# A staging buffer for transposed activations, three buffers instead of four for unit vectors, and narrower turns of half tiles

## The chip, the cores and the metric

The kernel runs on one core of one Trainium2 chip. The metric is the device time of one execution in microseconds, lower is better. TensorE does the matmuls, VectorE and ScalarE read PSUM and write SBUF, GpSimd (POOL) issues the loads of q, k, v and the weights and does a few additions, and SyncE (SP) issues the other DMAs.

## The reference

Cosine attention over 8 batches of 12 heads, 448 tokens and 64 numbers per head, then a mixing block on the 768 channels. Inputs and the output are float32; the kernel computes in bf16 with float32 sums.

```python
q_n = q / (norm(q) + 1e-6);  k_n = k / (norm(k) + 1e-6)     # q, k, v: (8, 12, 448, 64)
attn = softmax(q_n @ k_n.T / tau)                           # tau = 0.1
x = (attn @ v) -> (8, 448, 768)
u = x + transpose(transpose(x) @ U @ V)                     # U: 448 x 32, V: 32 x 448
out = u + relu(u @ w_ch1) @ w_ch2                           # 768 -> 3072 -> 768
```

## The kernel before

**Work and its tiles.** For each batch, q and k are loaded by thirds of four heads, squared and summed (lines 657 to 665), scaled to unit length (line 733), and transposed on TensorE pair of heads by pair (line 574, 112 columns). The transposed pair goes from PSUM into one of the buffers of `r_qkT` (line 397) by a copy on ScalarE (line 1475) or VectorE (line 1477). Scores are computed in bursts of up to three slots (line 797), exponentials on ScalarE (line 815), the product with v on TensorE (line 842), and its scaling on VectorE (lines 873 and 874), which writes into a tile `X` of the batch. There are two `X` buffers. In batches 2 and later the last quarter of the keys of two pairs is one slot, so that a burst may need three pairs.

`stage0` (line 947) then projects X with U (line 959), copies the 32-wide result A to SBUF, multiplies it with V (line 1012) and adds it to X on VectorE (line 1021): X now holds u. Every 128-token tile of u goes to DRAM twice, because the MLP comes later: as it is (`kept`, line 1050) and transposed (`turned`, line 1060). For the second one, TensorE turns the tile with six transposes of 128 columns (line 574 through `flip`), and a copy on ScalarE or VectorE writes the turned tile over the tile of X that it came from. Two batches make seven tiles, so the middle one (t = 3) is turned in two halves of 64 tokens, one for each batch. Batches 0 and 1 work partly in another way: batch 0's tiles aren't stored at all.

The MLP works on tiles of tokens: uT comes back from DRAM (line 908), u too (line 913). Tiles are taken two at a time, the down projection as seven half-size products (line 1328), the up projection plainly (line 1299) in the first six pairs of tiles and as seven products (line 1192) in the last six. The sums and differences of weights for the seven products live in space that earlier stages have left: `Gone` (line 57) makes them wait until the given-up buffers of the rings have had their last use. `Shrink` (line 37) is a ring that gives up buffers: `r_qkT` has six buffers for the first three batches (`NPAIR * WHOLE` = 18 pairs), and from then on those whose numbers are listed.

**What sets the order.** Nothing is emitted in the order of the source. The kernel records operations (`Op`) with an estimated duration, dependencies, and the ring slots that they take and give back; `Plan.run` (line 196) then walks through time and gives each engine its next operation. TensorE's operations stand in streams with a fixed rank (lines 502 to 512): transposes of q and k, then those of u (`pe_u`), then products with v, ..., scores, and the MLP last. An operation marked `ACT/DVE` goes to whichever of the two engines takes it first, and one marked `fast` waits for VectorE where that is free. So a change of one duration or one buffer changes the order of all engines from that place on, and the split of the shared operations. Each engine then executes its own list strictly in that order, and an operation that has to wait holds all behind it. What it waits for on the chip are the semaphores of the data it touches, not the slots of the plan.

For the turned tiles the plan of the kernel before says: the first transpose depends on the additions to u and on the store of u, `u_adds[x] + made[x][-1:]`. Only the copy, which writes over X, has to wait for that store on the chip.

Of the kernel before, what the change touches and what calls it, by code (L numbers as in the profile page):

```python
# [317 lines left out]
def kernel(  # L318
# [12 lines left out]
    nc = tc.nc  # L331

    B, H, S, D = q.shape
    C = H * D
    R = moe_U.shape[-1]
    F = moe_w_ch1.shape[-1]
    NPAIR = H // 2
    CC = C // 128
    NC = F // 128
    CH = C // 2  # L340
    SC = 4
    SCH = S // SC
# [9 lines left out]
    WHOLE = 3  # L352
# [21 lines left out]
    def fixed_ring(tiles):  # L374
        return Ring(len(tiles), lambda i: tiles[i % len(tiles)])
# [5 lines left out]
            for i in range(3)]  # L381
# [13 lines left out]
    r_inv = ring(4, [SCH, 2, G, SC], FP, "inv")  # L395
    qkT_t = sqk_t[:, 3 * SQ:]
    r_qkT = Shrink([qkT_t[:, 2 * SC * SCH * i:2 * SC * SCH * (i + 1)].rearrange("p (b s) -> p b s", b=2 * SC)
                    for i in range(6)], NPAIR * WHOLE, (2, 3, 4, 5))
    X_t = const.tile([128, 2 * 4 * C], BF, name="X_sb")
    r_X = fixed_ring([X_t[:, 4 * C * i:4 * C * (i + 1)].rearrange("p (t c) -> p t c", t=4) for i in range(2)])  # L400
    A_t = const.tile([128, 3, C], BF, name="A_sb")
# [49 lines left out]
    def bank_ring(groups, cap, shape=None):  # L451
        def make(g):
            if len(g) > 1:
                return bank_t[:, g[0]:g[-1] + 1, :]
            t_ = bank_t[:, g[0], :]
            if shape is not None:
                t_ = t_[:, 0:shape[0] * shape[1]].rearrange("p (a b) -> p a b", a=shape[0])
            return t_
        return BankRing(banks, groups, cap, make)
# [5 lines left out]
    r_z = bank_ring([(7,), (4,), (6,), (5,), (3,), (1,), (2,), (0,)], 4)  # L465
    r_sc = bank_ring([(0, 1), (2, 3), (4, 5)], 3)
    r_low = bank_ring([(5,), (4,), (3,), (2,), (1,), (0,)], 4)
    r_fl = bank_ring([(5,), (4,), (3,), (2,), (1,), (0,), (6,)], 2)
    r_av3 = bank_ring([(5,), (4,), (3,), (2,), (1,), (0,)], 2, (4, D + 8))
    r_av2 = bank_ring([(5,), (4,), (3,), (2,), (1,), (0,), (6,)], 2, (4, D + 8))  # L470
# [7 lines left out]
    r_sc1 = bank_ring([(0,), (2,), (1,), (3,)], 4)  # L478
# [4 lines left out]
    ident = const.tile([128, 128], BF, name="ident")  # L483
# [16 lines left out]
    plan = Plan()  # L500
# [6 lines left out]
    pe_u = plan.stream("PE")  # L507
# [11 lines left out]
    def pe_t(n):  # L519
        return n / 2400.0 + 0.0025  # L520

    def act_t(n, fixed=0.055):
        return fixed + n * 0.00083

    def dve_t(n, fast=1, fixed=0.065):
        return fixed + n * 0.00105 / fast

    def any_t(n, fast=1, fixed=0.065):
        return {"ACT": act_t(n), "DVE": dve_t(n, fast, fixed)}
# [32 lines left out]
    def flip(stream, ins, n, into, part, deps, acq, rel, wide=1, eng="ACT/DVE", took=0.05, ring_=None):  # L562


        tp = Slot(ring_ or r_mm, 1)
        tp.own = True
        for z, x in enumerate(ins):
            def fn(z=z, x=x):
                if z == 0:
                    w = len(ins) // wide  # L570
                    tp.tile = bank_t[:, tp.group[0], :].bitcast(BF)[:, 0:w * n].rearrange(
                        "p (w n) -> p w n", w=w)
                m = 128 // wide
                nc.tensor.transpose(out=tp.tile[m * (z % wide):m * (z % wide + 1), z // wide, :], in_=x(),  # L574
                                    identity=ident[:n, :n])
            o = plan.add(Op("PE", took, fn, deps=deps + [id_set] if z == 0 else (), acq=[tp] + acq,
                            rel=rel if z == len(ins) - 1 else []), stream)
        took = any_t(n * len(ins) // wide, 2)
        c = plan.add(Op(eng, took, None, deps=[o], acq=acq, rel=[tp], prio=0.2, fast=True))

        def move():
            for dst, src in part(into(), tp.tile):
                copy_op(c, dst, src)
        c.fn = move
        return c
# [304 lines left out]
    prev, first_v, made, u_adds, projects = {}, {}, {}, {}, {}  # L890
# [56 lines left out]
    def stage0(b, X, muls):  # L947
        par = b % 2
# [13 lines left out]
        def project_part(c0, c1, mm):  # L962
            for t in range(4):
                project(t, c0, c1, mm)
# [5 lines left out]
        if not by_pe:  # L970
            o = projects[b] = plan.add(Op("PE", 0.2 + 2 * pe_t(CH), project_all, deps=muls + consts[par], acq=mms + [A]), pe_a)
        for (c0, c1), mm in zip(cols, mms):
            need = [m for i, m in enumerate(muls) if i * D < c1]
            if by_pe:
                o = plan.add(Op("PE", 0.2 + pe_t(c1 - c0), lambda c0=c0, c1=c1, mm=mm: project_part(c0, c1, mm),
                                deps=need + consts[par], acq=[mm, A],
                                rel=[warm] if b == 0 and c0 == 0 else []),
                             pe_z[c0 // 128] if b == 0 else pe_a if c1 < C else pe_av)
# [7 lines left out]
        n = 128 * len(tiles)  # L986
# [12 lines left out]
        for jobs in (jobs, wide):  # L999
            for z, i, t, c0, c1 in jobs:  # L1000
# [7 lines left out]
                for y, (AA, col) in enumerate(parts):  # L1008
                    AA.uses += 1
                    AA.left += 1  # L1010
                    o = plan.add(Op("PE", pe_t(c1 - c0), lambda y=y, AA=AA, col=col, c0=c0, c1=c1,
                                    mm=mm, last=len(parts) - 1: nc.tensor.matmul(  # L1012
                        out=mm.tile[:, 0:c1 - c0], lhsT=V_sb[:, col:col + 128],
                        rhs=AA.tile[:, c0:c1], start=(y == 0), stop=(y == last)),
                        deps=(a_done if jobs is wide else [a_done[z]]) if y == 0 else (), acq=[mm] if y == 0 else [], rel=[AA]), pe_a if c1 < C or jobs is wide else pe_av)
# [10 lines left out]
                rel = [mm] + ([prev["X"]] if t == 3 and b == 1 else [])  # L1026
                for s_ in rel[1:]:
# [3 lines left out]
                                         deps=[o], rel=rel, prio=0 if b == 1 else 2))  # L1031
# [11 lines left out]
        for i, t in enumerate(tiles):  # L1043
            x = b // 2, t
            r = slice(64 * par, 64 * par + 64) if t == 3 and b > 1 else slice(0, 128)
            X.uses += 1
            X.left += 1
            u_adds[x] = [o for (z, k), o in adds.items() if k == i]
            made.setdefault(x, []).append(plan.add(Op(
                "SP", 0.1, lambda x=x, r=r, t=t: nc.sync.dma_start(out=kept[x][r, :], in_=X.tile[r, t - 3 * par, :]),  # L1050
                deps=u_adds[x], rel=[X], prio=1 if b == 1 else 0, lat=("x", 1.0, 2.0))))
            if x in turned:
                X.uses += 1
                X.left += 1
                view = lambda t=t: X.tile[:, t - 3 * par, :].rearrange("p (c n) -> p c n", c=CC)
                c = flip(pe_u, [(lambda cc=cc, t=t: X.tile[:, t - 3 * par, 128 * cc:128 * cc + 128]) for cc in range(CC)],
                         128, view, lambda t_, y, r=r: [(t_[:, :, r], y[:, :, r])], u_adds[x] + made[x][-1:], [], [],
                         took=0.056, ring_=r_sc1 if b == 1 else r_fl)
                made_t.setdefault(x, []).append(plan.add(Op(
                    "SP", 0.1, lambda x=x, r=r, view=view: nc.sync.dma_start(  # L1060
                        out=turned[x].rearrange("p (c n) -> p c n", c=CC)[:, :, r], in_=view()[:, :, r]),
                    deps=[c], rel=[X], prio=1 if b == 1 else 0, lat=("x", 1.0, 2.0))))
        prev["A"], prev["X"] = A, X
        return us, uT, ut

# [407 lines left out]
    def copy_op(op, dst, src):  # L1473
        if op.by == "ACT":
            nc.scalar.copy(out=dst, in_=src)  # L1475
        else:
            nc.vector.tensor_copy(out=dst, in_=src)
# [68 lines left out]
    def att(b):  # L1546
        X = Slot(r_X, 0) if b else X0
        muls = [] if b else list(muls0)
        for n, x in enumerate(groups_of(b) if b else ()):
            scores(b, x, first_v.get(b - 1, ()) if n == 0 and b == 2 else ())  # L1550
        for p in range(0 if b else 1, NPAIR):
            if b == 0:
                for c in range(SC):
                    scores(b, [(p, c)])
            muls += values(b, p, X)
        if b < WIDE <= b + 2:
            v_set[b + 2] = [fill(lambda: set_v_tiles(v_t[b % 2]), 1200, prio=3.5, deps=[last_av[b, p] for p in range(NPAIR)])]
        else:
            v_set[b + 2] = v_set[b]
        last_mul.extend(muls)  # L1560
        return stage0(b, X, muls)

    first = lead, [plan.add(Op("SP", 0.45, lambda i=i, src=src: nc.sync.dma_start(
        out=lead.tile[:, i], in_=src[0, 0:2].rearrange("h (s c) d -> s h (c d)", c=SC)),
        acq=[uv], prio=-5, lat=2.5)) for i, src in enumerate((q, k))]
# [8 lines left out]
    for c in range(SC):  # L1574
# [8 lines left out]
                        deps=[zf, *begun], prio=-2, lat=12.0))]  # L1583
# [37 lines left out]
    n = 0  # L1621
# [68 lines left out]
```

## Time and profile before

| | us |
|---|---|
| median of 3 runs (lowest, highest) | 572.73 (572.58, 574.4) |
| the profiled execution | 573.77 |
| its span, first to last instruction | 572.0 |
| TensorE busy | 561.3 |
| VectorE busy | 464.3 |
| ScalarE busy | 306.2 |
| POOL busy | 148.5 |

A row of the profile names the line, the engine, the operation and the tiles, then the time it was busy, the mean duration of one, and the engine's idle time before it with what ended that. Line numbers are those of the kernel before; PE is TensorE, DVE VectorE, ACT ScalarE, SPq SyncE's queue. Line 574 is shared by all transposes, and lines 1475 and 1477 by all copies that either engine may take, so the tile's name and the shape tell them apart. The granted TensorE clock is 1.00 throughout.

### The profile page before, as it was taken

The page shows a single profiled execution, that of the slowest core. Times are in us where ns is not written, and L with a number is a line of the kernel's source. Part 1 is how long each engine was busy: PE and PEld are TensorE (multiplying, and loading weights), DVE is VectorE, ACT ScalarE, POOL GpSimd, SP SyncE. Part 2 cuts the span into 40 slices and gives each one's busy share as a digit, 9 for nine tenths or more (in the row PEclk, how much of TensorE's full clock was granted, in tenths as well). Part 3 has the DMA queues.
Part 4 walks back from the last instruction along what each step waited for, and adds up shares of the span by engine and source line. Part 5 has one row for each costly group of instructions (what it writes and reads, how often), then busy time and mean ns, then how long its engine had stood idle before and what let it go on. Part 6 is the DMA issues. An engine that isn't in the chain of part 4 may idle for free.

```text
span 572.0 us, 16131 instructions
## 1 busy us (share of the span) xinstructions
PE 561.3 (98%) x6721; PEld 412.7 (72%) x6722; DVE 464.3 (81%) x1061; ACT 306.2 (54%) x495; POOL 148.5 (26%) x180
## 2 busy tenths in 40 slices
PE   8899999999999999999999999999999999999996
PEld 6565656768767758767867766876969696969784
DVE  8979859999898989979969976687897776758583
ACT  7977655766567874766865684560404141414140
POOL 8526241002424225124120510001030303030302
PEclk9999999999999999999999999999999999999999
DMA  9999997632968849349645922312124121221201
GB/s 156 204 207 139 210 192 107 144 84 52 105 155 128 87 88 177 64 93 136 95 83 101 131 70 71 112 30 84 30 78 127 37 83 31 83 69 45 79 7 55
DMA packets 116264, 57.61 MB, mean 101 GB/s; under 512 B 72256, under 2 KB 116192, under 8 KB 116192
## 3 DMA queue, kind: packets, MB, share of 16 engines
q0 software_dynamic: 72352, 25.73, 39.8%
q1 hardware_dynamic: 43840, 30.87, 18.8%
q8 instruction: 52, 0.85, 0.6%
q14 instruction: 20, 0.16, 0.1%
HBM read 61.65 MB, written 20.64 MB: 144 GB/s over the span
## 4 chain that ended last, share of the span: by engine, by line
PE 91%; DVE 5%; ACT 1%; DMA 1%; issue 1%; POOL 0%; SPq 0%; DVEq 0%; POOLq 0%
PE bank L1328 28%; PE bank L1299 16%; PE bank L1192 15%; PE bank L842 8%; PE bank L797 6%; PE bank L1411 6%; PE bank L1453 6%; PE bank L574 5%; DVE qk_all L733 2%; PE bank L1012 1%; DVE ss L665 1%; PE bank L959 1%; DMA relu<-in_k_dram 1%; DVE X_sb L1021 0%; DMA out_dram<-relu 0%
## 5 line engine op out<-in xcount | busy, mean ns | idle before, releaser
L815 ACT ACTIVATE attn<-bank 128x896 bf16<-128x896 f32 (+1 forms) x163 | 140.1, 915 | 35.8 <-PE bank L797 35.3
L1328 PEld LDWEIGHTS <-relu 128*128 128x128 bf16 x1008 | 95.5, 98 | 66.2 <-issue 7.7
L1299 PE MATMUL bank<-uT,w_sb 128*128 128x256 bf16 x864 | 106.1, 273 | 1.6 <-ACT relu L1309 1.4
L1328 PE MATMUL bank<-w_sb,relu 128*128 128x384 bf16 x576 | 103.4, 326 | 0.0
L1299 PEld LDWEIGHTS <-w_sb 128*128 128x128 bf16 x864 | 81.0, 98 | 20.3 <-issue 9.9
L665 DVE TENSOR_REDUCE ss<-sqk 112x8 f32<-112x512 bf16 x95 | 62.1, 675 | 3.1 <-ACT sqk L657 2.6
L733 DVE TENSOR_TENSOR qk_all<-qk_all,inv 112x512 bf16<-112x512 bf16 x93 | 60.5, 683 | 0.3
L842 PE MATMUL bank<-v_nat,attn 128*128 128x65 bf16 (+1 forms) x1536 | 58.3, 193 | 0.8 <-DVE X_sb L880 0.6
L842 PEld LDWEIGHTS <-attn 128*128 128x128 bf16 (+1 forms) x1536 | 53.8, 97 | 5.4 <-issue 3.3
L596 POOL DMA_DIRECT2D qk_all<-in_q_dram x24 | 17.7, 738 | 147.9 <-ACT attn L815 49.1
L1309 ACT ACTIVATE relu<-bank 128x512 bf16<-128x512 f32 x48 | 28.7, 598 | 44.1 <-PE bank L1299 43.3
L1192 PEld LDWEIGHTS <-w_sb 128*128 128x128 bf16 x864 | 49.3, 98 | 0.8
L797 PE MATMUL bank<-sqk 64*64 64x448 bf16 (+1 forms) x460 | 46.9, 356 | 0.7 <-ACT sqk L1475 0.5
L1229 ACT COPY attn<-bank 128x512 f32<-128x512 f32 x18 | 10.6, 587 | 65.6 <-PE bank L1192 60.6
L1220 ACT ACTIVATE relu<-relu 128x512 bf16<-128x512 bf16 x36 | 22.7, 630 | 29.7 <-DVE relu L1214 28.8
L1192 PE MATMUL bank<-uT,w_sb 128*128 128x128 bf16 x648 | 38.1, 219 | 0.0
L1353 POOL TENSOR_TENSOR relu<-relu,u_nat 128x384 f32<-128x384 f32 x7 | 8.4, 1205 | 110.0 <-ACT relu L1351 82.7
L1411 PE MATMUL bank<-uT,w_sb 128*128 128x384 bf16 (+1 forms) x288 | 35.6, 273 | 0.0
L619 POOL DMA_DIRECT2D v_nat<-in_v_dram x42 | 31.1, 746 | 17.2 <-DMA w_sb<-in_moe_w_ch_dram 14.6
L1453 PE MATMUL bank<-w_sb,relu 128*128 128x384 bf16 x192 | 35.4, 326 | 0.0
L874 DVE TENSOR_TENSOR X_sb<-bank,rd 128x256 bf16<-128x256 f32 x72 | 30.6, 425 | 2.6 <-DVE rd L873 0.2
L1353 POOL TENSOR_TENSOR attn<-attn,u_nat 128x384 f32<-128x384 f32 x6 | 12.8, 2156 | 69.0 <-ACT attn L1351 69.0
(137 smaller groups left out, 943.2 us busy)
## 6 DMA issues: line engine op xcount, KB each, us to landing
qk_all<-in_q_dram POOLq DMA_DIRECT2D x23, 224.0 KB, 4.2
qk_all<-in_k_dram POOLq DMA_DIRECT2D x23, 224.0 KB, 5.5
u_nat<-u SPq DMA_DIRECT2D x25, 192.0 KB, 2.5
w_sb<-in_moe_w_ch_dram POOLq DMA_DIRECT2D x4, 1152.0 KB, 17.9
w_sb<-in_moe_w_ch_dram POOLq DMA_DIRECT2D x8, 576.0 KB, 15.5
uT<-uT SPq DMA_DIRECT2D x24, 192.0 KB, 3.0
u<-X_sb SPq DMA_DIRECT2D x22, 192.0 KB, 2.0
uT<-X_sb SPq DMA_DIRECT2D x21, 192.0 KB, 3.1
```

Of the source, the lines that this page charges most:

```text
L619: ops = [load(lambda j=j, r0=r0, c=c, s0=s0, s1=s1: nc.gpsimd.dma_start(out=v_t[b % 2][r0:r0 + s1 - s0, :, j, 0:D], in_=src[c, s0:s1]), (s ...
L665: lambda i=i, a0=a0, a1=a1, sq=sq: nc.vector.reduce_sum(ss.tile[:, i, a0:a1, :].rearrange("p h c -> p (h c)"), sq.tile[:, 0:a1 - a0, :].re ...
L733: (nc.gpsimd if pool_ else nc.vector).tensor_mul(dst, src, sc)
L797: nc.tensor.matmul(out=out, lhsT=qkT.tile.rearrange("p b s -> p (b s)")[r, n0:n0 + w], rhs=qkT.tile[r, SC:2 * SC, :].rearrange("p c s -> p ...
L815: exps.append(plan.add(Op("ACT", act_t(2 * S, 0.058), lambda sc=sc, c=c, attn=attn: nc.scalar.activation(out=attn.tile[:, :, off:off + S] ...
L842: nc.tensor.matmul(out=av.tile[:, t, 0:D + 1], lhsT=tail.tile[:, hh, 128 * t:128 * (t + 1)] if tail and j == SC - 1 else (attn if j < SC - ...
L874: nc.vector.tensor_mul(X.tile[:, :, h * D:(h + 1) * D], av.tile[:, :, 0:D], rd.tile.to_broadcast([128, 4, D]))
L1192: o = plan.add(Op("PE", pe_t(128), lambda i=i, j=j, jj=jj: nc.tensor.matmul(out=mm.tile[:, 128 * jj:128 * jj + 128], lhsT=left[k](i, j), r ...
L1299: o = plan.add(Op("PE", pe_t(256), lambda j=j, e=e, cc=cc, mm=mm: nc.tensor.matmul(out=mm.tile[:, 256 * e:256 * e + 256], lhsT=w1_sb[:, cc ...
L1328: o = plan.add(Op("PE", pe_t(CH), lambda j=j: nc.tensor.matmul(out=mm.tile[:, 0:CH], lhsT=left[k](j), rhs=right[k](j), start=(first and j ...
L1411: o = plan.add(Op("PE", pe_t(n), lambda cc=cc: nc.tensor.matmul(out=mm.tile[:, m:m + n], lhsT=w1_sb[:, cc, f * 128:(f + 1) * 128], rhs=uT. ...
L1453: nc.tensor.matmul(out=mm.tile[:, 0:c1 - c0], lhsT=relu.tile[:, f, i * 128:(i + 1) * 128], rhs=w2_t[:, f, c0:c1], start=(f == 0), stop=(f ...
```

## The change

Three things are changed, in two places of the code.

- For batches 2 to 6 (`1 < b < B - 1`) the turned tile is written into a new ring `r_st` of one buffer and no longer over X. It lies where buffer 2 of `r_qkT` was. The transposes depend on the additions alone, give X back when they end, and take the slot of `r_st`, which is given back by the store of the turned tile. Batch 7 and batch 1 stay in place.
- From batch 3 on `r_qkT` has the buffers 3, 4 and 5, and no longer 2.
- A half tile is turned by six ordinary matmuls against 64 columns of the identity, into float32 in PSUM, in place of six transposes of 128 columns into bf16. This holds for the half tiles of batches 2 to 7. The bank for it comes from `r_fl`.

```diff
-                    for i in range(6)], NPAIR * WHOLE, (2, 3, 4, 5))
+                    for i in range(6)], NPAIR * WHOLE, (3, 4, 5))
...
+    r_st = fixed_ring([qkT_t[:, 2 * 2 * SC * SCH:2 * 2 * SC * SCH + C].rearrange("p (c n) -> p c n", c=CC)])
...
-                view = lambda t=t: X.tile[:, t - 3 * par, :].rearrange("p (c n) -> p c n", c=CC)
-                c = flip(pe_u, [(lambda cc=cc, t=t: X.tile[:, t - 3 * par, 128 * cc:128 * cc + 128]) for cc in range(CC)],
-                         128, view, lambda t_, y, r=r: [(t_[:, :, r], y[:, :, r])], u_adds[x] + made[x][-1:], [], [],
-                         took=0.056, ring_=r_sc1 if b == 1 else r_fl)
+                aside = 1 < b < B - 1
+                st = Slot(r_st, 1) if aside else None
+                view = (lambda st=st: st.tile) if aside else lambda t=t: X.tile[:, t - 3 * par, :].rearrange("p (c n) -> p c n", c=CC)
+                need, took, gave = (u_adds[x], [st], [X]) if aside else (u_adds[x] + made[x][-1:], [], [])
+                if r == slice(0, 128):
+                    c = flip(pe_u, [(lambda cc=cc, t=t: X.tile[:, t - 3 * par, 128 * cc:128 * cc + 128]) for cc in range(CC)],
+                             128, view, lambda t_, y: [(t_, y)], need, took, gave,
+                             took=0.056, ring_=r_sc1 if b == 1 else r_fl)
+                else:
+                    tp = Slot(r_fl, 1)
+                    for cc in range(CC):
+                        o = plan.add(Op("PE", 0.0295, lambda cc=cc, t=t, tp=tp, r=r: nc.tensor.matmul(
+                            out=tp.tile[:, 64 * cc:64 * cc + 64], lhsT=X.tile[:, t - 3 * par, 128 * cc:128 * cc + 128],
+                            rhs=ident[:, r], start=(cc == 0), stop=(cc == CC - 1), skip_group_check=True),
+                            deps=need if cc == 0 else [], acq=[tp, *took] if cc == 0 else [], rel=gave if cc == CC - 1 else []), pe_u)
+                    c = plan.add(Op("ACT/DVE", any_t(CH), None, deps=[o], rel=[tp], prio=0.2, fast=True))
+                    c.fn = lambda c=c, tp=tp, r=r, view=view: copy_op(
+                        c, view()[:, :, r], tp.tile[:, 0:CH].rearrange("p (c n) -> p c n", c=CC))
                 made_t.setdefault(x, []).append(plan.add(Op(
                     "SP", 0.1, lambda x=x, r=r, view=view: nc.sync.dma_start(
                         out=turned[x].rearrange("p (c n) -> p c n", c=CC)[:, :, r], in_=view()[:, :, r]),
-                    deps=[c], rel=[X], prio=1 if b == 1 else 0, lat=("x", 1.0, 2.0))))
+                    deps=[c], rel=[st or X], prio=1 if b == 1 else 0, lat=("x", 1.0, 2.0))))
```

## The prediction

> **What bounds the kernel now.** I read the page's engine sums first, then the sums by stretch, then the chain of work that ended last.
>
> ```profile
> span 572.0 us, 16131 instructions
> PE 561.3 (98%) x6721; PEld 412.7 (72%) x6722; DVE 464.3 (81%) x1061; ACT 306.2 (54%) x495; POOL 148.5 (26%) x180
> PE 91%; DVE 5%; ACT 1%; DMA 1%; issue 1%; POOL 0%; SPq 0%; DVEq 0%; POOLq 0%
> 149.00:211.90 62.90, 62.88 (x710) 43.81 (x703) 55.13 (x129) 45.52 (x72) 19.49 (x26) 1.00 0.70 112
> 211.90:259.00 47.10, 46.95 (x567) 33.77 (x565) 41.47 (x99) 29.86 (x48) 13.82 (x19) 1.00 0.69 110
> 259.00:305.00 46.00, 46.00 (x568) 33.58 (x567) 38.18 (x92) 31.94 (x50) 13.86 (x19) 1.00 0.72 110
> 305.00:354.50 49.50, 47.94 (x578) 34.53 (x577) 39.60 (x94) 31.21 (x49) 10.95 (x15) 1.00 0.54 89
> ```
>
> The columns of a stretch are its length, then PE, PEld, DVE, ACT and POOL busy, clock, DMA share, GB/s. TensorE sets the end: it is idle 0.0 to 0.2 us in three of the four stretches where batches 3 to 6 are computed, at full clock (1.00). So a microsecond of TensorE work removed is worth a microsecond, as long as the other engines keep up. VectorE is next: 55.13 of 62.90 us, 88%, in the first. The fourth stretch alone shows a hole, 49.50 − 47.94 = 1.56 us. The chain of work there (start, length, what):
>
> ```profile
> 325.52 0.34 PE bank L574 x6
> 325.86 0.79 PE bank L842 x26
> 326.65 0.16 PE bank L1012
> 326.81 1.76 PE bank L1299 x16
> 328.57 0.02 issue
> 328.59 0.80 ACT X_sb L1475
> 329.39 0.51 ACT relu L1309
> 329.90 0.04 issue
> 329.94 0.60 PE bank L1299 x4
> ```
>
> TensorE transposed a tile of u at 325.52 and ran out of work at 328.57, because a relu was late. That relu stood in ScalarE's queue behind the copy of the turned tile, which ran only at 328.59. The rows of the timeline and of the stores of u (line 1050) from 320 to 330 us tell why:
>
> ```profile
> 328.59 0.80 ACT L1475 COPY X_sb<-bank 128x768 bf16<-128x768 bf16 x1 [3.40 <-PE bank L1299]
> 321.56 0.33 SPq L1050 DMA_DIRECT2D u<-X_sb  x1
> DMA to landing us min/median/max: 2.0/4.5/7.0
> ```
>
> The copy writes over the tile in place, so it waits for the store of u. That store, issued at 321.56 and 7.0 us on its way, landed at 328.56. The releaser named in the bracket is not the real one. At 317 to 329 us ten loads of v fill the DMA engines; two stores of turned tiles begun in that time took 6.0 and 4.6 us, where stores beside no loads of q, k or v took 1.8 to 2.4.
>
> **Part 1, half tiles turned by 64 columns.** Six half tiles (batches 2 to 7, six matmuls each) were turned 128 columns wide. The chain prices both widths: 0.34 us / 6 = 57 ns for 128 columns (line 574), 0.79 / 26 = 30.4 ns for 65 columns (line 842). Saved: 6 × (0.34 − 6 × 0.0304) = 0.95 us, all on TensorE, which is the path. The other counts of TensorE are the same in the built order of both kernels. A rule speaks against it: the Trainium skill, "TensorE: Matmul & The Clock Gate", section "Back-to-back issue gap", has weight load and matmul together set the spacing, about 81 ns per pair at 128 columns. By that rule, with an unchanged 128-column weight load per half-tile matmul, nothing would be saved (0.00 instead of −0.95). The row decides: at line 842 every matmul has its own load, and the pairs run at 30 ns. I take −0.95; bounds 0 and −0.95.
>
> The copy of such a half now reads float32 instead of bf16: on VectorE as line 1477 to A_sb (551 ns) instead of to X_sb (355), on ScalarE 487 for 474. Six copies, under 0.7 us together, off the path; they are in the load below.
>
> **Part 2, no wait for the store of u.** For batches 2 to 6 the copy goes to a buffer of its own. The hole goes: 329.94 − 328.57 = 1.37 us on the path. Bounds: −1.56 (the stretch's whole idle time) and 0 (the relu is then late by something else). I take −1.37, as nothing else stood ahead of that relu. X is released when the transposes end and not when its store lands: no wait for a free X shows in the waits, so 0.
>
> **Part 3, the wait that is added.** There is one such buffer, so each copy waits until the previous turned tile has landed in DRAM. This wait stands on the copying engine: VectorE for 14 of the 20 tiles in the changed order, ScalarE for 6. Queued behind a held copy on VectorE are mostly the reciprocal and scaling of the next head (lines 873, 874), whose bank the next values matmuls need; on ScalarE a relu or an exponential, as in the hole above. In the changed order two copies within a batch stand some 5.6 to 6.2 us of TensorE work apart (two pairs 4.7). A copy takes 0.55 us (VectorE) or 0.80, its store follows after 0.03 us and lands in 1.8 to 6.0 us, median 3.1: 2.4 to 6.8 us in all. At the median there is no wait. Within the v loads (12 us per batch, so about two tiles) 0.55 + 0.03 + 5.5 = 6.1 us against 5.8: some 0.3 us of wait each, up to 2 us at 4.7 us apart. For four batches: 8 × 0.3 = 2.4 us of held queues. How much reaches TensorE? In the kernel before, most of TensorE's waits are met 0.3 to 1.5 us early, so a quarter: +0.6. Bounds 0 and +2.4. On the SP queue a store of a turned tile waits for its copy; behind it stand loads of uT for a later pair of tiles and output stores. The kernel before waited 0.2 us once for such a load (173 us), so 0. Stores and loads are as many as before, and POOL's queue is unchanged.
>
> **Part 4, three buffers for transposed unit vectors.** A burst of scores holds up to three pairs, as the last quarter of the keys is shared by two, so three buffers just suffice. A pair's transposes stand behind the burst that frees its buffer. In the changed order the least TensorE work from the end of such transposes to the scores that read them is 2.4 us; before, 2.6. Needed are 0.26 us to the copy's start and 0.62 (VectorE) or 0.91 us (ScalarE): 1.2 at most. So 0, covered by MLP matmuls; with that cover gone a burst would come up to 1.2 us late. The weight differences that take over the freed third buffer run long after its last use in batch 2: 0.
>
> **Part 5, work moved to VectorE.** The new order also hands flexible work around. VectorE gets 7 squares, 4 relus, 2 copies of unit vectors and 2 of A more, and the copies of u change from 14 whole and 3 half to 15 and 3 float32 halves:
>
> ```profile
> L661 DVE TENSOR_TENSOR sqk<-qk_all 112x512 bf16<-112x512 bf16 x41 | 16.0, 417 | 0.2
> L1311 DVE TENSOR_SCALAR relu<-bank 128x512 bf16<-128x512 f32 x24 | 16.5, 688 | 8.7 <-PE bank L1299 8.6
> L1477 DVE COPY sqk<-bank 128x896 bf16<-128x896 bf16 x18 | 11.1, 618 | 6.3 <-PE bank L574 6.2
> L1477 DVE COPY X_sb<-bank 128x768 bf16<-128x768 bf16 x14 | 7.6, 553 | 2.1 <-PE bank L574 1.5 <-issue 0.5
> L1477 DVE CAST A_sb<-bank 128x384 bf16<-128x384 f32 x3 | 1.7, 551 | 0.0
> ```
>
> 7 × 0.417 + 4 × 0.688 + 2 × 0.618 + 2 × 0.551 + (15 × 0.553 + 3 × 0.551 − 14 × 0.553 − 3 × 0.355) = 2.92 + 2.75 + 1.24 + 1.10 + 1.14 = 9.1 us. ScalarE loses some 10. In the four stretches VectorE was busy 174.4 of 205.5 us, 85%; with 9.1 more, 89%. From the projection of batch 2 to that of batch 3 (152.1 to 212.2, 60.1 us) its summed work goes from 56.0 to 57.9 us, 96%. The cover is VectorE's idle time, 31 us in the four stretches. Between 149 and 412 us TensorE already loses about 1.2 us to late VectorE and ScalarE results, in pieces of 0.1 to 0.35 us by the starts of its matmuls in the timeline, apart from the hole. I take four tenths more: +0.5. Bounds: −0.4 (the pieces happen to fall better) and +9.1 (no idle time can be used).
>
> **The sum.** The profiled execution took 573.77 us: span 572.0 and 1.77 around it. 572.0 − 0.95 − 1.37 + 0.6 + 0.5 = 570.8 of span, 572.5 with what lies around. The median of the runs, 572.73, is 1.04 below the profiled one, so 571.5 for the median, 0.2% less.
>
> **Rivals.**
> - *Better than summed.* The new buffer's waits and VectorE's load stay hidden: 572.73 − 2.3 = 570.4. For it: VectorE's 31 us idle. Against: 96% in batch 3's stretch.
> - *The wait changes its place.* A store of a turned tile takes 6 to 7 us among the v loads, and holds the next copy as the store of u did. One such hold at TensorE's cost of the old one: −0.95 − 1.37 + 0.6 + 1.37 + 0.5, so 572.9. For it: 6.03 us measured for a store of a turned tile at 317.7. Against: the copies stand 5.6 us apart or more.
> - *Narrow matmuls save nothing* (the rule above): 571.5 + 0.95 = 572.4. Against: line 842.
> - *VectorE becomes the bound; slower.* VectorE works in a fixed order and its idle time is waiting for TensorE, ScalarE and DMA; if that can't be used, the 9.1 us come through from batch 3 to 6. At one half: 572.73 − 2.32 + 4.6 = 575.0. The forecast turns slower from 25% on (2.32 / 9.1), by more than 0.3% from 44% on. For it: 93% busy already in batch 3's stretch, 96% after. Against: 80 to 88% in the others.
>
> **How the numbers follow.** A measurement of this kernel tells about 0.3% (1.7 us) from no change. The sum: 0.44, its own range 569.9 to 573.0, below 571.0 in 0.19 and within in 0.25. Better than summed: 0.15, faster. The wait moved: 0.10, and narrow matmuls without gain: 0.04, both within. VectorE: 0.27, slower, 574.5 to 578. So faster 0.34, within 0.39, slower 0.27. The range 569.8 to 575.8 leaves out the upper part of the VectorE case (0.13) and a little below.
>
> **What would show it.** Part 1: 36 matmuls of 64 columns, six in 0.18 us. Part 2: no copy of a turned tile that waits 3 us, and no TensorE hole at its relu. Part 3: idle time ahead of the copies into the new buffer, 2 to 3 us in total, with stores of 5 us and more before them. Part 4: no TensorE idle time ahead of scores released by a copy of unit vectors. Part 5: VectorE 9 us busier, and TensorE's idle time in the four stretches still under 3 us. It is wrong if that idle time grows past 4 us (VectorE), or if the hole comes back behind another store.

## The result, and the profile after

The changed kernel took 570.99 us in the median of its five runs (570.67 to 571.51), the kernel before 573.38 in the five beside them (572.58 to 574.4). The ratio is 0.9953, with a 95% interval of 0.994 to 0.9966: 0.47% faster; the two medians lie 2.4 us (0.42%) apart. By the interval that is more than the 0.3% which the prediction set as its bound. The kernel before had a median of 572.73 to 574.13 in the sets of runs of this study, so below only ratios within one set are compared.

The profiled execution took 570.67 us with a span of 568.9, against 573.77 and 572.0 before. What lies around the span is 1.8 us in both, so the span alone has the difference, 3.1 us. That of before lies 0.4 us above its kernel's median and the other 0.3 us below its own, so 0.7 of the 3.1 us comes from which executions were profiled.

The page's span, engine sums and shares of the chain:

```profile
span 568.9 us, 16133 instructions
PE 559.2 (98%) x6721; PEld 411.4 (72%) x6722; DVE 473.7 (83%) x1077; ACT 298.1 (52%) x479; POOL 148.3 (26%) x180
PE 94%; DVE 4%; ACT 1%; DMA 1%; POOL 0%; issue 0%; DVEq 0%; POOLq 0%
```

The sums by stretch of batches 3 to 6 (length, then PE, PEld, DVE, ACT and POOL busy with the number of instructions, clock, DMA share, GB/s; cut at this kernel's own projections, so that they are 203 us in all and not 205.5):

```profile
149.00:211.00 62.00, 62.00 (x707) 43.09 (x700) 56.51 (x128) 41.47 (x65) 19.30 (x26) 1.00 0.68 109
211.00:258.00 47.00, 46.95 (x562) 34.15 (x561) 43.58 (x103) 28.82 (x45) 13.83 (x19) 1.00 0.68 108
258.00:304.00 46.00, 46.00 (x569) 33.48 (x567) 41.03 (x98) 28.52 (x45) 12.38 (x17) 1.00 0.71 111
304.00:352.00 48.00, 47.96 (x581) 34.63 (x579) 42.85 (x101) 30.95 (x48) 12.59 (x17) 1.00 0.61 98
```

TensorE's idle time in the fourth stretch fell from 1.56 us to 0.04: the hole is gone. VectorE became 9.4 us busier (464.3 to 473.7), and 91% busy in the four stretches (56.51 + 43.58 + 41.03 + 42.85 = 183.97 of 203), yet TensorE is idle for only 0.1 us in the four together.

The groups that answer to those shown of before, with the half tiles' matmuls and weight loads first (line 1067 is new; 661 has become 662, 1311 is 1326, 1475 is 1490, 1477 is 1492):

```profile
L1067 PE MATMUL bank<-ident,X_sb 128*128 128x64 bf16 x36 | 2.0, 192 | 0.0
L1067 PEld LDWEIGHTS <-X_sb 128*128 128x128 bf16 x36 | 1.7, 97 | 0.4
L662 DVE TENSOR_TENSOR sqk<-qk_all 112x512 bf16<-112x512 bf16 x48 | 18.8, 416 | 0.9 <-DMA qk_all<-in_q_dram 0.9
L1326 DVE TENSOR_SCALAR relu<-bank 128x512 bf16<-128x512 f32 x28 | 19.2, 686 | 5.3 <-PE bank L1314 5.3
L1492 DVE COPY sqk<-bank 128x896 bf16<-128x896 bf16 x20 | 12.4, 618 | 2.5 <-PE bank L575 2.4
L1490 ACT CAST sqk<-bank 128x384 bf16<-128x384 f32 x2 | 1.0, 478 | 2.1 <-DMA uT<-sqk 1.7 <-PE bank L1067 0.4
```

The last row is a copy into the new buffer (the profile calls it sqk, after the tensor that it lies in). Its bracket names the added wait: 1.7 us, for the store of the turned tile before. It is the only copy so held. In the timeline of ScalarE:

```profile
280.94 2.54 ACT L816 ACTIVATE attn<-bank 128x896 bf16<-128x896 f32 x3 [0.93 <-PE bank L798]
285.18 0.48 ACT L1490 CAST sqk<-bank 128x384 bf16<-128x384 f32 x1 [1.70 <-DMA uT<-sqk]
285.66 0.60 ACT L1324 ACTIVATE relu<-bank 128x512 bf16<-128x512 f32 x1
```

The store ahead of it was issued at 278.6 us and took 6.46. TensorE has no wait there: the relu at 285.66, held behind the copy, was still in time. Of all stores of turned tiles (line 1075) the page of that line says:

```profile
DMA to landing us min/median/max: 1.8/2.3/6.5
```

**Where the 3.1 us came from.** A wait of TensorE is here the time by which a matmul starts later than its usual spacing behind the one before it, by the starts in the timeline; those over 0.1 us from 100 us on are counted (earlier ones, the largest 0.33 us at 95 us, are alike in all kernels). The kernel before has nine, 3.06 us in all: the hole, 1.55 at 329.9, and eight of 0.10 to 0.34. The kernel after has four, 0.66 us: 0.22 at 215.2, 0.20 at 311.6, 0.14 at 241.4 and 0.10 at 143.4. So 1.55 (hole) + 0.85 (small waits) = 2.40. The narrow turns save 0.95 by the prediction's sum, and make it 3.35 of 3.1 measured.

The same sum over all kernels of this study shows how far it can be trusted. "Rest" is the span less the waits, plus 0.95 where half tiles are turned narrow:

| kernel | span | waits (largest) | rest |
|---|---|---|---|
| before | 572.00 | 3.06 (1.55) | 568.94 |
| after | 568.87 | 0.66 (0.22) | 569.16 |
| no_hold | 570.38 | 1.21 (0.33) | 569.17 |
| half_only | 572.29 | 3.52 (1.31) | 569.72 |
| half_same | 570.98 | 3.00 (0.96) | 568.93 |
| three_only | 570.09 | 1.07 (0.59) | 569.02 |
| stage_only | 570.75 | 1.79 (0.95) | 568.96 |
| three_half | 568.98 | 0.78 (0.19) | 569.15 |
| price_031 | 569.33 | 0.79 | 569.49 |
| price_056 | 569.49 | 1.61 | 568.83 |
| wide_same | 570.03 | 0.56 | 569.47 |
| dve_1 | 569.89 | 1.49 | 569.35 |
| twice | 580.04 | 9.93 (4.20) | 571.06 |
| dve_3 | 589.76 | 17.57 | 573.14 |

But for the last two, the rest lies between 568.8 and 569.7 us. So, within half a microsecond either way, the kernel's time is a fixed amount of TensorE work plus these waits, and a smaller term isn't settled by this sum. Each row is one execution.

### The profile page after: what moved, and what is told of

It reads as the page before. It is cut to its first block, busy times and chain, and to the rows that moved or that the text cites. A ratio compares the mean times of both kernels' runs of the same rounds, so it can differ in the third digit from the quotient of the medians.

```text
span 568.9 us, 16133 instructions
## 1 busy us (share of the span) xinstructions
PE 559.2 (98%) x6721; PEld 411.4 (72%) x6722; DVE 473.7 (83%) x1077; ACT 298.1 (52%) x479; POOL 148.3 (26%) x180
## 4 chain that ended last, share of the span: by engine, by line
PE 94%; DVE 4%; ACT 1%; DMA 1%; POOL 0%; issue 0%; DVEq 0%; POOLq 0%
PE bank L1343 29%; PE bank L1314 17%; PE bank L1207 15%; PE bank L843 8%; PE bank L798 6%; PE bank L1426 6%; PE bank L1468 6%; PE bank L575 4%; PE bank L1013 2%; DVE qk_all L734 1%; PE bank L960 1%; DVE ss L666 1%; DMA relu<-in_q_dram 1%; POOL sqk L660 0%; DVE X_sb L881 0%
## 5 line engine op out<-in xcount | busy, mean ns | idle before, releaser
L1314 PE MATMUL bank<-uT,w_sb 128*128 128x256 bf16 x864 | 104.9, 273 | 0.0
L1324 ACT ACTIVATE relu<-bank 128x512 bf16<-128x512 f32 x44 | 26.3, 597 | 43.9 <-PE bank L1314 38.8
```

The source lines that it names most:

```text
L1314: o = plan.add(Op("PE", pe_t(256), lambda j=j, e=e, cc=cc, mm=mm: nc.tensor.matmul(out=mm.tile[:, 256 * e:256 * e + 256], lhsT=w1_sb[:, cc ...
```

## The experiments

The first theory was the prediction's own: the narrow turns and the vanished hole make the gain, and the new buffer is what removes the hole. The rival was that some other part, or merely the new order, does it. The first four runs share 35 runs of the kernel before (median 573.58).

**no_hold: the kernel before, where nothing waits for the store of u.** In batches 2 to 6 the store sends a piece of the weights, of the same size, to the place of u. So u itself isn't stored there, and the copy over X has no store to wait for; the order of all engines is unchanged.

```diff
-                "SP", 0.1, lambda x=x, r=r, t=t: nc.sync.dma_start(out=kept[x][r, :], in_=X.tile[r, t - 3 * par, :]),
+                "SP", 0.1, lambda x=x, r=r, t=t: nc.sync.dma_start(out=kept[x][r, :], in_=w1_sb[r, 0, 0:C] if 1 < b < B - 1 else X.tile[r, t - 3 * par, :]),
```

> The kernel before, its order on TensorE, VectorE, ScalarE and POOL unchanged; only the stores of u of batches 2 to 6 read the first 768 columns of the weights of the up projection in place of X, so the copy that writes over X no longer waits for a store (u is stored wrong, the sizes and times of the stores stay). My theory (the store of u among the loads of v holds ScalarE's queue): the TensorE hole at 328.6 to 329.9 us goes, 1.4 us less than before, 0.998 of its time. Rival (the relu was late by something else, or TensorE's time comes back later): no change, 1.000.

Measured: 572.16 us, ratio 0.998 (0.997 to 0.9989), span 570.4, 1.6 less than before. The timeline of ScalarE:

```profile
325.82 0.80 ACT L1475 COPY X_sb<-bank 128x768 bf16<-128x768 bf16 x1 [0.70 <-PE bank L574]
327.21 0.60 ACT L1309 ACTIVATE relu<-bank 128x512 bf16<-128x512 f32 x1 [0.59 <-PE bank L1299]
```

And the fourth stretch:

```profile
305.00:354.50 49.50, 49.33 (x598) 35.33 (x596) 40.40 (x96) 31.99 (x50) 10.95 (x15) 1.00 0.54 89
```

The copy that ran at 328.59 before now runs at 325.82, right after its transposes, the relu is no longer late, and the stretch's idle time falls from 1.56 us to 0.17. In an unchanged order, that shows that the store of u made the hole. Its worth is 1.4 us by the medians, 1.6 by the spans, and 0.6 to 1.7 by the interval of the ratio.

**half_only: narrow turns alone, order free to change.** On the changed kernel:

```diff
-                    for i in range(6)], NPAIR * WHOLE, (3, 4, 5))
+                    for i in range(6)], NPAIR * WHOLE, (2, 3, 4, 5))
...
-                aside = 1 < b < B - 1
+                aside = False
```

> The kernel before with the half tiles turned by 64 columns alone: turned in place, four buffers for unit vectors. The sum: 36 matmuls at 30 instead of 57 ns, 0.95 us less, and whatever the new order does to small waits (0.5 either way); the hole by a store of u may stay or move. Rival (the weight load sets the pace of narrow matmuls): no change from this part.

Measured: 574.08 us, ratio 1.0013 (1.0003 to 1.0023), span 572.3. It became slightly slower: the interval leaves out no change. The matmuls of line 1067 start 29 ns apart, as in the changed kernel. But the planner gave another order, with new holes. The timeline of ScalarE:

```profile
233.45 0.80 ACT L1490 COPY X_sb<-bank 128x768 bf16<-128x768 bf16 x1 [2.79 <-DMA u<-X_sb]
234.15 1.09 ACT L1324 ACTIVATE relu<-bank 128x512 bf16<-128x512 f32 x2
```

The second stretch, in which TensorE is now idle for 1.91 us:

```profile
211.90:259.00 47.10, 45.19 (x552) 32.91 (x551) 41.34 (x100) 30.71 (x51) 13.83 (x19) 1.00 0.69 105
```

Another copy is now held 2.79 us, and here the bracket names the store of u itself; the relu behind it cost TensorE 1.31 us at 234.8. Two waits of 0.94 and 0.83 us came elsewhere. So a part of this change can't be priced by running it alone: each part gives the planner another order.

**three_only: three buffers for unit vectors alone.** On the kernel before:

```diff
-                    for i in range(6)], NPAIR * WHOLE, (2, 3, 4, 5))
+                    for i in range(6)], NPAIR * WHOLE, (3, 4, 5))
```

> The kernel before with three instead of four buffers for transposed unit vectors, nothing else. My sum puts 0 on it, with up to 0.5 us either way from the changed order. Rival (a score burst comes late for want of a buffer): some 40 bursts of batches 3 to 7, each late by up to 1.2 us, several us slower and TensorE idle time ahead of line 797.

Measured: 572.16 us, ratio 0.9978 (0.9965 to 0.999), span 570.1. The part that I had put down at 0 is faster by itself. Its order still holds a copy behind a store of u, for less long (timeline of ScalarE):

```profile
330.89 0.91 ACT L1475 COPY sqk<-bank 128x896 bf16<-128x896 bf16 x1
332.87 0.80 ACT L1475 COPY X_sb<-bank 128x768 bf16<-128x768 bf16 x1 [1.08 <-DMA u<-X_sb]
333.57 1.09 ACT L1309 ACTIVATE relu<-bank 128x512 bf16<-128x512 f32 x2
```

That cost TensorE 0.59 us. All waits together are 1.07 us, two thirds less than before.

**stage_only: the changed kernel with half tiles turned by 128 columns into bf16.**

```diff
-                if r == slice(0, 128):
+                if True:
...
-                             128, view, lambda t_, y: [(t_, y)], need, took, gave,
+                             128, view, lambda t_, y, r=r: [(t_[:, :, r], y[:, :, r])], need, took, gave,
```

> The changed kernel with the half tiles turned by 128 columns again: the buffer for turned tiles and three buffers for unit vectors without the narrow turns. If the parts add up, 0.95 us slower than the changed kernel, so some 1.4 us (0.25%) faster than before. Rival (the gain over the sum comes from the chance of the order): anything from 1 us better to 1.5 us worse than that, with TensorE idle time at other places.

Measured: 572.59 us, ratio 0.9986 (0.9977 to 0.9994), span 570.7. That is 1.9 us over the changed kernel's span: 0.95 of wider turns and 1.13 of waits (1.79 for 0.66) less 0.2 of rest. The largest wait, 0.95 us, is for a relu on VectorE. The chain there:

```profile
220.98 0.12 PE bank L1314
221.10 0.02 issue
221.13 0.70 DVE relu L1326
221.83 0.04 issue
221.87 0.49 PE bank L1314 x3
```

The relu began 0.03 us after the last matmul that it reads, so nothing held it, no store either: in this order TensorE's next matmuls wait for the relu. So the new buffer does not keep TensorE fed by itself; three_only, without it, had fewer waits.

The next four runs share 11 runs of the kernel before (median 574.13). They measure the disputed sizes on the changed kernel with its order kept.

**wide_same: the same order, the half tiles turned by 128 columns.** The six results overlap in PSUM, so the turned half tile isn't the right one.

```diff
-                            out=tp.tile[:, 64 * cc:64 * cc + 64], lhsT=X.tile[:, t - 3 * par, 128 * cc:128 * cc + 128],
-                            rhs=ident[:, r], start=(cc == 0), stop=(cc == CC - 1), skip_group_check=True),
+                            out=tp.tile[:, 64 * cc:64 * cc + 128], lhsT=X.tile[:, t - 3 * par, 128 * cc:128 * cc + 128],
+                            rhs=ident, start=(cc == 0), stop=(cc == CC - 1), skip_group_check=True),
```

> The changed kernel in its own order, only that each of the 36 matmuls of half tiles streams 128 columns of the identity in place of 64 (the columns then overlap in PSUM, so the turned halves are wrong; the copies are unchanged). My sum: 36 x 26.5 ns = 0.95 us slower than the changed kernel, ratio to before 0.997 instead of 0.9953, and the spacing at that line 56 instead of 30 ns. Rival (the weight load sets the pace): no change, 0.9953.

Measured: 571.76 us, ratio 0.9961 (0.9948 to 0.9974), span 570.0. The chain of this kernel, and then of the changed one, at the same half tile:

```profile
221.93 0.40 PE bank L575 x8
222.33 0.34 PE bank L1067 x6
222.67 0.97 PE bank L843 x32
```

```profile
221.54 0.40 PE bank L575 x8
221.94 0.17 PE bank L1067 x6
222.11 0.97 PE bank L843 x32
```

Six matmuls take 0.34 us at 128 columns and 0.17 at 64. By their starts the spacing is 56 against 29 ns, so 36 × 27 ns = 0.97 us, and the span is 1.16 us longer. The narrow turns are worth what the sum said. It is the spacing that shows this: the ratios to before, 0.9961 and 0.9953, differ by less than their intervals.

**twice: the store of every turned tile issued twice.**

```diff
-                    "SP", 0.1, lambda x=x, r=r, view=view: nc.sync.dma_start(
-                        out=turned[x].rearrange("p (c n) -> p c n", c=CC)[:, :, r], in_=view()[:, :, r]),
+                    "SP", 0.1, put,
...
+                def put(x=x, r=r, view=view, n=2 if aside else 1):
+                    for _ in range(n):
+                        nc.sync.dma_start(
+                            out=turned[x].rearrange("p (c n) -> p c n", c=CC)[:, :, r], in_=view()[:, :, r])
```

> The changed kernel, the store of each turned tile of batches 2 to 6 issued twice from the new buffer, so that the next copy waits for both. Plan and order otherwise unchanged; 20 stores of 192 KB or 96 KB more. The buffer comes free some 0.4 to 2 us later than the 1.8 to 6.5 us measured, against copies 4.7 to 6.2 us apart. If the wait for the buffer is as tight as my +0.6 us said, several more copies stand and TensorE loses 1 to 2 us; if it is covered, under 0.5 us.

Measured: 581.81 us, ratio 1.0133 (1.0116 to 1.0151), span 580.0, 11.2 over the changed kernel. The expectation was far too low. Timeline of SyncE's queue, then of VectorE:

```profile
232.78 6.02 SPq L1076 DMA_DIRECT2D uT<-sqk  x2
238.89 0.38 SPq L1051 DMA_DIRECT2D u<-X_sb  x1
```

```profile
243.12 0.56 DVE L1495 COPY sqk<-bank 128x768 bf16<-128x768 bf16 x1 [6.50 <-issue]
243.59 0.68 DVE L1329 TENSOR_SCALAR relu<-bank 128x512 bf16<-128x512 f32 x1
```

Two issues that take 0.3 us each need 6.02 here, as the second store, to the same place in DRAM, was issued only when the first had landed: in the trace SyncE waits for the semaphore of the first store just before the second, so the program itself puts them in a row. The first took 5.64 us from 232.8, the second 4.47 from 238.5: the buffer was taken for 10.2 us. The next copy stood 6.50 us at the head of VectorE's list, the relu behind it was late, and TensorE waited 4.20 us at 244.3. So the mechanism of the added wait is real, and it reaches TensorE once a buffer stays taken for long. As SyncE's later work was held too, this run doesn't give the cost of a doubled transfer alone. Part of its 11.2 us is not a wait either. The sums by stretch right after that wait:

```profile
244.40:247.80 3.40, 3.40 (x21) 2.32 (x22) 3.30 (x10) 0.00 (x0) 0.00 (x0) 0.50 0.32 116
```

TensorE is busy throughout at half the clock (0.50). The trace has this clock for 3.41 us, so some 1.7 us were lost (an estimate, half of it), which brings this kernel's rest of 571.06 us down to 569.4, among the others.

**dve_1 and dve_3: VectorE loaded further.** For batches 3 to 6, one or three small multiplications on a tile that nothing else reads there, ahead of every scaling of a head; nothing else is changed (`dve_3` has `3` for the `1`).

```diff
+                    for _ in range(1 if 2 < b < B - 1 else 0):
+                        nc.vector.tensor_mul(warm_t, warm_t, warm_t)
```

> The changed kernel with one more VectorE multiply of 128 bf16 ahead of each of the 48 head scalings of batches 3 to 6, outside the plan: some 48 x 0.2 = 9 us more VectorE work, as much as the change itself moved there. My term: a twentieth comes through, under 1 us. Rival (VectorE is the bound): half and more, 4 us and up.

> The same with three such multiplies per head, some 28 us more VectorE work, with about 21 us of VectorE idle time left in those batches in the changed kernel. If VectorE's idle time can be used, some 7 to 12 us slower; if it can't, near 28 us. With the run with one multiply this gives the load from which VectorE decides.

Measured: 571.62 us, 0.9958 (0.9944 to 0.9973), and 591.63 us, 1.0306 (1.0292 to 1.0321). The engine sums of dve_1, then of dve_3:

```profile
PE 559.8 (98%) x6721; PEld 411.5 (72%) x6722; DVE 478.8 (84%) x1125; ACT 298.4 (52%) x479; POOL 148.3 (26%) x180
```

```profile
PE 566.9 (96%) x6721; PEld 412.0 (70%) x6722; DVE 499.8 (85%) x1221; ACT 299.3 (51%) x479; POOL 148.3 (25%) x180
```

VectorE is 5.1 and 26.1 us busier than in the changed kernel (473.7); the added multiplications alone have records of 11.2 and 34.0 us in sum, which overlap with others. The spans are 1.0 and 20.9 us longer: a fifth and four fifths of the busy time come through. The first figure is uncertain: TensorE's waits rose from 0.66 to 1.49 us, but the ratio, 0.9958 for 0.9953, is the changed kernel's within the intervals. The 20.9 us lie between the two forecasts for dve_3. So VectorE had room left for this change's 9.4 us, and little beyond: with 26 us more it is close to being the bound.

By now the theory said that the buffer keeps the waits short, as three_only and stage_only had each lost only a part. The next three share 11 runs of before (median 574.01) and ask whether the gain needs the buffer, and whether it is a matter of one lucky order.

**three_half: the changed kernel without the new buffer**, copies going over X again.

```diff
-                aside = 1 < b < B - 1
+                aside = False
```

> The changed kernel without its buffer: half tiles turned by 64 columns and three buffers for unit vectors, but turned in place behind the store of u, as before. Account so far: span = some 569.1 us - 0.95 for narrow turns + TensorE's waits of over 0.1 us after 60 us (2.96 us before, 0.66 in the changed kernel, 1.08 with three buffers alone, 3.5 with narrow turns alone). If the buffer is what keeps these waits short, they are 1.5 us and more here, with a copy held by a store of u, and the kernel is 1 us or more slower than the changed one (ratio to before 0.997 and up). Rival (the chance of the order): waits under 1 us, equal to the changed kernel.

Measured: 571.07 us, ratio 0.9955 (0.9939 to 0.9972), span 569.0; the changed kernel has 0.9953. The page's span and engine sums:

```profile
span 569.0 us, 16142 instructions
PE 560.0 (98%) x6721; PEld 412.0 (72%) x6722; DVE 467.7 (82%) x1065; ACT 305.6 (54%) x491; POOL 148.2 (26%) x180
```

The fourth stretch, with no idle time of TensorE:

```profile
304.00:352.00 48.00, 48.00 (x586) 34.34 (x587) 42.22 (x100) 29.51 (x46) 12.38 (x17) 1.00 0.60 97
```

My theory fell: the whole gain is there without the buffer. In this order no store of u holds a copy, though each copy still has to wait for one: each of batches 2 to 6 began within 0.1 us of the end of its transposes or of the work before it on its engine. The closest store landed 0.14 us before its copy, at 236.9 us. And VectorE has 6 us less work than in the changed kernel.

**price_031 and price_056: other orders of the changed kernel.** The duration that the planner assumes for a half-tile matmul is raised; the instructions stay, their order changes (`price_056` has `0.056`).

```diff
-                        o = plan.add(Op("PE", 0.0295, lambda cc=cc, t=t, tp=tp, r=r: nc.tensor.matmul(
+                        o = plan.add(Op("PE", 0.031, lambda cc=cc, t=t, tp=tp, r=r: nc.tensor.matmul(
```

> The changed kernel, its planner told 31 instead of 29.5 ns for a narrow turn: the same instructions in a slightly other order. If the buffer keeps waits short whatever the order, TensorE's waits after 60 us stay under 1 us and the time within 0.1% of the changed kernel (ratio 0.995 to 0.9965). If the changed kernel's 0.66 us are chance, 1 to 3 us of waits.

> The same with the old price of 56 ns, a larger shift of the order. Same numbers: under 1 us of waits if the buffer settles it, 1 to 3 us if the order does.

Measured: 571.1 us, 0.9949 (0.9933 to 0.9964), and 571.22 us, 0.9955 (0.994 to 0.9969); waits of 0.79 and 1.61 us. The gain is not that of one order: three of the changed kernel give the same within the intervals, and none is clearly better than the changed kernel. The buffer doesn't keep the waits short whatever the order, though: the 1.61 us are what was expected if the order decides.

**half_same: narrow turns alone, in the order of the kernel before.** Since half_only had changed the order, the planner is here given the old durations, and so writes the same order on every engine as in the kernel before.

```diff
-                    for i in range(6)], NPAIR * WHOLE, (3, 4, 5))
+                    for i in range(6)], NPAIR * WHOLE, (2, 3, 4, 5))
...
-                aside = 1 < b < B - 1
+                aside = False
...
-                        o = plan.add(Op("PE", 0.0295, lambda cc=cc, t=t, tp=tp, r=r: nc.tensor.matmul(
+                        o = plan.add(Op("PE", 0.056, lambda cc=cc, t=t, tp=tp, r=r: nc.tensor.matmul(
...
-                    c = plan.add(Op("ACT/DVE", any_t(CH), None, deps=[o], rel=[tp], prio=0.2, fast=True))
+                    c = plan.add(Op("ACT/DVE", any_t(2 * CH, 2), None, deps=[o], rel=[tp], prio=0.2, fast=True))
```

> Narrow turns alone, in place, four buffers, and the planner told the old prices, so that the order of all engines is that of the kernel before. By the account, narrow turns are worth 0.95 us in whatever order, and the 2.1 us more that narrow turns alone lost (waits of 3.5 instead of 2.96 us and the rest) came from that run's order: 0.9 to 1.0 us less than before, ratio 0.998 to 0.9985, with the hole at 329 us still there (1.4 to 1.6 us). Rival (narrow turns make a later wait grow by what they save): no change, ratio 1.000, and a hole of 2 us and more.

Measured: 573.19 us in the median of 12 runs, 574.08 of before in 17; ratio 0.9995 (0.9983 to 1.0008), span 571.0. The medians are 0.9 us apart and the spans 1.0, as expected, but the interval includes no change: by the ratio this run is inconclusive, and the spacing in wide_same is what settles the size. Its waits moved. The timeline of ScalarE:

```profile
327.72 0.80 ACT L1490 COPY X_sb<-bank 128x768 bf16<-128x768 bf16 x1 [2.37 <-PE bank L1314]
```

The first and the fourth stretch:

```profile
149.00:211.90 62.90, 62.11 (x704) 43.29 (x696) 54.69 (x127) 44.89 (x71) 19.51 (x27) 1.00 0.70 112
305.00:354.50 49.50, 48.82 (x593) 35.10 (x589) 40.11 (x95) 31.94 (x49) 10.92 (x15) 1.00 0.53 88
```

The held copy runs 0.87 us earlier than before and its hole is 0.51 us, while the first stretch has a new wait of 0.96 us, for a load of uT at 174. In an unchanged order, the hole's size is that of a race between a store and the queue behind it.

## Why the prediction was right and wrong

The time, 570.99 us, lies within the range, and the direction of the forecast was right, though the prediction held a change under 0.3% likelier (0.39) than a faster kernel (0.34). That it is only 0.5 below the forecast is partly luck: the forecast's base was a median of 572.73, and beside the result the kernel before had 573.38. The difference of medians is 2.4 us where the sum gave 1.2. In size it is the rival "better than summed" (2.3).

- **Part 1 held.** −0.95 was taken; 36 matmuls of 64 columns were found, six in 0.17 us, and wide_same shows 0.97. The rule of the Trainium skill ("TensorE: Matmul & The Clock Gate", section "Back-to-back issue gap"), about 81 ns for a weight load and a matmul of 128 columns, is contradicted here: every one of the 36 has its own load of 128 columns, with a record of 97 ns, and they start 29 ns apart, 56 at 128 columns. So the loads overlap with other matmuls. That nothing would be saved at 64 columns was the prediction's own reading of the rule.
- **Part 2: the mechanism of the hole was right, the credit was not.** no_hold shows that the store of u held the copy, and the copy the relu. −1.37 was taken, 1.55 was lost there. But the step credits the new buffer with ending this. three_half has none and no hole, because its order lets each store land before the copy is due. The dependence was there and cost nothing.
- **Part 3 was mis-sized.** +0.6 was taken, from about 0.3 us of wait at each of eight copies, a quarter of which reaches TensorE. Measured was one held copy, 1.70 us, and nothing on TensorE. The term rested on eight stores of some 5.5 us within the loads of v; of the 20 stores from the new buffer five took over 4 us, and only behind the one of 6.46 did a copy have to wait. That one hold is the rival "the wait changes its place" without its cost. The prediction's 1.8 to 2.4 us for stores beside no loads of q, k or v was too narrow a reading: in the trace of before four such stores of turned tiles took 3.3 to 4.0. The step's warning was justified all the same: twice shows what becomes of it at 10.2 us.
- **Part 4 was right about the wait, wrong about the order.** From batch 2 on no matmul of scores waited for a copy of unit vectors (one does at 13.8 us, 0.5 us in both kernels). But the buffer's loss also changes the order, and three_only is 1.9 us of span faster.
- **Part 5 failed in the step from load to waits.** VectorE got 9.4 us more where 9.1 was summed, and the copies of u are 15 whole and 3 half, as said. But +0.5 was taken, as four tenths more of the existing 1.2 us of small waits (1.41 by the starts), and the waits besides the hole fell instead, from 1.51 us in the whole kernel to 0.66. That is −0.85, below even the lower bound of −0.4. In a fixed order the load does cost (dve_3: 26.1 us more, 20.9 us of span); what outweighed it here is that the new order has fewer late results. The prediction took the waits to follow from the load alone; at this load they follow first from the order.
- **The rival that ends slower** (VectorE the bound) turned slower at a quarter of the load coming through. Of 9.4 us nothing visible came through, of 5.1 more at most about a fifth, of 26.1 more four fifths. It was not the wrong mechanism, only not reached.

With the measured terms: 572.0 − 0.95 − 1.55 + 0.0 − 0.85 = 568.65 of span, for 568.87. Two of the prediction's terms, +0.6 and +0.5, came out at 0.0 and −0.85, and neither error shows in the hit.

What stays open: three kernels with four buffers and stores that can hold a copy (before, half_only, half_same; two orders, as half_same has that of before) had 3.0 to 3.5 us of waits. Those with three buffers and no added load (after, three_only, stage_only, three_half, price_031, price_056, wide_same) had 0.56 to 1.79, in six orders (wide_same has that of after). Why three buffers should give shorter waits, or whether six related orders happened to fall well, these runs don't tell. Four unit-vector buffers with the new buffer beside them were not tried.

## What to carry to other kernels

Where one engine is 98% busy, write its time as fixed work plus the list of its own late starts, each with its place and what was late: that sum held within half a microsecond over twelve kernels here, and it tells at once whether an edit removed work or a wait. In a kernel whose order is planned, every edit deals all engines a new order worth up to 3 us, so try a part in an order that is held fixed (change the operand, the source of a store, or the planner's price, not the structure), and don't add up parts that were run alone. An operation that waits for a DMA holds all that stands behind it on its engine; before buying a buffer for it, see whether a change of order lets the DMA land in time.

## What was not expected of the hardware

- A store of a 192 KB turned tile took from 1.8 to 6.5 us in one kernel. In the changed kernel the four from the new buffer that took over 4 us (4.16 to 6.46) all lie beside loads of q and k, three of them beside loads of v too; but a half tile, 96 KB, took 4.36 us beside four stores of u and no load of q, k or v.
- In `twice` the granted TensorE clock fell to 0.50 for 3.41 us, from 244.4 us on, as TensorE took up work after its wait of 4.20 us. After the next longest wait there, some 2 us at 344.7, it stayed at 1.00, as it did in every stretch of the other kernels shown here. Where between these two lengths the clock gives way, or whether length alone decides it, these runs don't tell.
